# Loading the last two rows of an output projection apart on five load queues, and widening its matmuls to 512 columns

## The chip, the cores and the metric

One NeuronCore of one Trainium2 chip. The metric is device time in microseconds (us); every time quoted is a median over executions of one kernel, with their number where it matters. All differences here are below 3%, most below 1%, so each comparison uses runs of the kernel before taken on the same chip (the record names no chip for the first pair). The diffs of the experiments are shortened, and those of e6 and e7 are written against the changed kernel for reading.

## The reference, cut to what matters

Two decode steps of attention, A and B, are independent and their rows are concatenated. Each has 32 heads of 128, one query row, and an output projection `wo` of 4096 x 512 in bf16. A reads 16384 keys, B only the last 4096.

```
o = softmax(q k^T / sqrt(128)) v          # per head, one row of 128
out = o.reshape(1, 32 * 128) @ wo         # 1x4096 @ 4096x512, for A and for B
```

## The kernel before

The kernel streams 352 MB of K, V and weights through one DMA queue row (16 hardware queues, which work in parallel) and computes behind it. The change touches only the end: loading `wo` and multiplying by it. `wo`'s 4096 rows lie 32 to a partition (J = 32). A "row a partition" below is one j: 128 rows of `wo`, one on each partition, and one matmul of contraction depth 128 with a one-column weight.

```python
def _load_wo(nc, cx, st, j0, n):
    ...
    src = st.wo.rearrange("(p j) f -> p j f", j=J)
    cx.o(nc.sync.dma_start(out=st.wo_t[:, j0 : j0 + n, :], in_=src[:, j0 : j0 + n, :]))

def _fin_rows(nc, cx, sts):
    ...                                   # orow: 64 partitions, one head each; A on 0-31, B on 32-63
    for st in sts:                        # spread each head's 128 values over 4 partitions: oc_ps
        ...

def _out(nc, cx, st, j0, n):
    if j0 == 0:
        st.oc = cx.singles.tile([P, J], BF16, ...)
        cx.o(nc.vector.tensor_copy(st.oc[:, :], st.oc_ps[:, 0:J]))
    if cx.out_ps is None:
        cx.out_ps = cx.red_pool.tile([P, 2, 512], F32, tag="red", name="out_ps")
    w = st.DN // st.cols
    out = [cx.out_ps[r : r + 1, b, 0:w] for r, b in st.out_at]
    for j in range(j0, j0 + n):
        for x in range(st.cols):          # A: 1 x 512 columns; B: 2 x 256
            cx.o(nc.tensor.matmul(
                out[x], lhsT=st.oc[:, j : j + 1], rhs=st.wo_t[:, j, x * w : (x + 1) * w],
                start=(j == 0), stop=(j == J - 1),
            ))
    if j0 + n == J:
        row = ...
        cx.o(nc.vector.tensor_copy(row[0:1, 0:w], out[0]))
        if st.cols == 2:
            cx.o(nc.scalar.copy(row[0:1, w:], out[1]))
        cx.o(nc.sync.dma_start(out=cx.out[...], in_=row[0:1, :]))

# in problem():  row and bank of PSUM for the halves of the output row
st.out_at = ((0, 0),) if name == "A" else ((64, 0), (96, 1))
# pieces, in load order:  A 16, 16;  B 16, 8, 4, 2, 2
for p in pieces:
    _out(nc, cx, *p)                      # all of A, then all of B, in load order
```

The softmax here doesn't subtract the row's maximum and nothing guards it: scores larger than these inputs give would overflow.

## Time and profile before

| | before |
|---|---|
| time, median of 4 | 823.43 us (822.85 to 824.11) |
| profiled span | 821.2 us |
| DMA | 352 MB, 429 GB/s over the span |
| TensorE busy | 37% |
| last piece of B's `wo` landed | 818.16 us |
| last matmul done | 818.59 us |

From the page of the kernel before: the span, TensorE's busy share, and the row of the DMA engines' mean busy share in 40 equal slices of the span (9 is 90% or more), and the instruction fetches (packets, MB, share).

```profile
span 821.2 us, 4767 instructions
...
PE 301.1 (37%) x2148; PEld 117.3 (14%) x2148; DVE 600.7 (73%) x146; ACT 35.1 (4%) x133; POOL 1.3 (0%) x9
...
DMA  9999999999999999999999999999999999999997
...
q8 instruction: 16, 0.26, 0.1%
```

The DMA row is 9 in all slices but the last: the load stream bounds the kernel, and the change is aimed at its tail. The end of the chain of waits of the kernel before (start us, us, what) shows that tail.

```profile
789.00 29.16 DMA wo_t<-in_B_wo_dram
...
818.21 0.43 PE out_ps L307 x4
818.63 0.41 DVE rowB L316
```

The last piece of `wo` lands, four matmuls and a cast follow, then the output DMA of 1 KB. TensorE's part of the same stretch, from the timeline of the kernel before (start us, us, engine, line, operation, out<-in, shape, count, what ended the idle time before it):

```profile
803.73 8.75 PE L307 MATMUL out_ps<-wo_t,ocA 128*1 128x512 bf16 x32 [0.25 <-DVE ocA L300]
...
813.35 1.91 PE L307 MATMUL out_ps<-wo_t,ocB 128*1 128x256 bf16 x32 [0.87 <-DVE ocB L300]
...
815.69 1.04 PE L307 MATMUL out_ps<-wo_t,ocB 128*1 128x256 bf16 x16 [0.43 <-DMA wo_t<-in_B_wo_dram]
...
818.21 0.38 PE L307 MATMUL out_ps<-wo_t,ocB 128*1 128x256 bf16 x4 [0.29 <-DMA wo_t<-in_B_wo_dram]
818.62 0.42 DVE L316 CAST rowB<-out_ps 1x256 bf16<-1x256 f32 x1 [5.32 <-PE out_ps L307]
818.65 0.37 ACT L318 CAST rowB<-out_ps 1x256 bf16<-1x256 f32 x1 [15.50 <-PE out_ps L307]
```

B's 32 half-row matmuls of the first piece took 1.91 us, so a row of 512 columns costs about 0.12 us; A's 32 whole-row matmuls took 8.75 us, over a stretch in which the clock was at half for 3.4 us. And TensorE waits for a DMA before each later piece of B: it has room.

What the change aims at is visible only in the trace's record of DMA landings. A load's 16 queues each report when their share has landed. Sorted, for B's last piece in the kernel before (us):

```
814.96 815.09 815.11 815.21 815.31 815.47 815.65 815.92 | 817.77 817.88 817.92 817.98 817.99 818.10 818.10 818.16
```

Eight queues are done 1.85 us before the first of the other eight. The late half makes the kernel wait.

### The profile page before, as it was taken

The page shows a single profiled execution, that of the slowest core. Times are in us where ns is not written, and L with a number is a line of the kernel's source. Part 1 is how long each engine was busy: PE and PEld are TensorE (multiplying, and loading weights), DVE is VectorE, ACT ScalarE, POOL GpSimd, SP SyncE. Part 2 cuts the span into 40 slices and gives each one's busy share as a digit, 9 for nine tenths or more (in the row PEclk, how much of TensorE's full clock was granted, in tenths as well). Part 3 has the DMA queues.
Part 4 walks back from the last instruction along what each step waited for, and adds up shares of the span by engine and source line. Part 5 has one row for each costly group of instructions (what it writes and reads, how often), then busy time and mean ns, then how long its engine had stood idle before and what let it go on. Part 6 is the DMA issues. An engine that isn't in the chain of part 4 may idle for free.

```text
span 821.2 us, 4767 instructions
## 1 busy us (share of the span) xinstructions
PE 301.1 (37%) x2148; PEld 117.3 (14%) x2148; DVE 600.7 (73%) x146; ACT 35.1 (4%) x133; POOL 1.3 (0%) x9
## 2 busy tenths in 40 slices
PE   3433705143223415060606151423414250606076
PEld 1111202011011102020202020101101020202033
DVE  2099895997496867799196949599659677689921
ACT  0100000000010000000001000000001000000010
POOL 0000000000000000000000000000000000000000
PEclk9855668586767677675858585857666676768599
DMA  9999999999999999999999999999999999999997
GB/s 383 434 457 412 456 412 454 412 454 418 427 442 444 425 441 429 441 416 447 421 445 437 431 435 434 432 423 443 441 418 451 425 445 421 448 413 455 413 424 317
DMA packets 8235, 352.62 MB, mean 429 GB/s; under 512 B 916, under 2 KB 920, under 8 KB 1304
## 3 DMA queue, kind: packets, MB, share of 16 engines
q1 hardware_dynamic: 8212, 352.33, 99.3%
q8 instruction: 16, 0.26, 0.1%
q14 instruction: 3, 0.02, 0.0%
q10 hardware_dynamic: 4, 0.00, 0.0%
HBM read 352.32 MB, written 0.00 MB: 429 GB/s over the span
## 4 chain that ended last, share of the span: by engine, by line
DMA 61%; issue 15%; DVE 13%; PE 11%; ACT 0%; SPq 0%; DVEq 0%
DMA kt<-in_A_k_cache_dram 42%; DMA vt<-in_A_v_cache_dram 12%; PE red L190 7%; DVE kt L178 6%; DVE kt L169 4%; PE acc L231 4%; DMA vt<-in_B_v_cache_dram 4%; DMA wo_t<-in_B_wo_dram 4%; DVE sc L206 2%; ACT p_sb L212 0%; SPq L115 0%; PE out_ps L307 0%; DVE rowB L316 0%; DVEq L169 0%
## 5 line engine op out<-in xcount | busy, mean ns | idle before, releaser
L169 DVE TENSOR_TENSOR kt<-kt,qallA 128x32768 bf16<-128x32768 bf16 (+2 forms) x20 | 276.2, 13810 | 162.5 <-DMA kt<-in_A_k_cache_dram 162.5
L231 PE MATMUL acc<-vt,p_sb 128*8 128x512 bf16 (+1 forms) x1280 | 113.0, 530 | 444.4 <-ACT p_sb L212 344.4
L178 DVE TENSOR_TENSOR kt<-kt 128x16384 bf16<-128x16384 bf16 (+2 forms) x24 | 174.3, 7261 | 0.2
L190 PE MATMUL red<-kt,ident 128*128 128x512 bf16 x640 | 151.2, 396 | 54.6 <-DVE kt L178 54.6
L231 PEld LDWEIGHTS <-p_sb 128*8 128x8 bf16 (+1 forms) x1280 | 37.6, 112 | 515.7 <-ACT p_sb L212 419.8
L190 PEld LDWEIGHTS <-ident 128*128 128x128 bf16 x640 | 63.0, 101 | 142.2 <-issue 47.1
L169 DVE TENSOR_TENSOR kt<-kt,qallB 128x16384 bf16<-128x16384 bf16 x8 | 69.5, 8686 | 2.9 <-DMA kt<-in_B_k_cache_dram 2.9
L206 DVE TENSOR_REDUCE sc<-red 128x256 f32<-128x2048 f32 x20 | 45.7, 2284 | 5.6 <-PE red L190 5.6
L212 ACT ACTIVATE p_sb<-sc,offA 128x256 bf16<-128x256 f32 x32 | 16.0, 500 | 574.7 <-DVE sc L206 574.7
L245 DVE TENSOR_TENSOR acc<-acc,maskA 128x512 f32<-128x512 f32 x16 | 11.1, 694 | 21.4 <-PE acc L231 21.4
L212 ACT ACTIVATE p_sb<-sc,offB 128x128 bf16<-128x128 f32 x32 | 12.4, 388 | 161.2 <-DVE sc L206 161.2
L130 PE MATMUL q_ps<-wq_t,scr 128*128 128x512 bf16 x64 | 15.7, 407 | 6.9 <-DMA wq_t<-in_A_wq_dram 4.9
L251 DVE TENSOR_REDUCE s<-acc 128x128 f32<-128x512 f32 x24 | 16.6, 691 | 0.8
L307 PE MATMUL out_ps<-wo_t,ocA 128*1 128x512 bf16 x32 | 8.8, 443 | 0.3 <-DVE ocA L300 0.3
L245 DVE TENSOR_TENSOR acc<-acc,maskB 128x512 f32<-128x512 f32 x8 | 5.5, 692 | 4.5 <-PE acc L231 4.5
L130 PEld LDWEIGHTS <-scr 128*128 128x128 bf16 x64 | 6.5, 103 | 15.6 <-issue 8.0
L316 DVE CAST rowA<-out_ps 1x512 bf16<-1x512 f32 x1 | 0.7, 678 | 8.8 <-PE out_ps L307 8.8
L259 PE MATMUL f_ps<-s,selA 128*32 128x128 f32 x32 | 6.5, 285 | 0.0
L212 ACT ACTIVATION_READ_ACCUMULATOR p_sb<-sc,offA 128x1 f32 x32 | 6.0, 187 | 0.0
L212 ACT ACTIVATION_READ_ACCUMULATOR p_sb<-sc,offB 128x1 f32 x32 | 6.0, 186 | 0.0
L307 PE MATMUL out_ps<-wo_t,ocB 128*1 128x256 bf16 x64 | 4.3, 272 | 1.8 <-DMA wo_t<-in_B_wo_dram 0.9
L102 DVE CAST scr<-xT 128x128 bf16<-128x128 f32 (+1 forms) x6 | 2.1, 459 | 3.6 <-PE xT L94 3.5
(43 smaller groups left out, 26.4 us busy)
## 6 DMA issues: line engine op xcount, KB each, us to landing
kt<-in_B_k_cache_dram SPq DMA_DIRECT2D x8, 4096.0 KB, 32.4
vt<-in_B_v_cache_dram SPq DMA_DIRECT2D x8, 4096.0 KB, 23.8
wq_t<-in_A_wq_dram SPq DMA_DIRECT2D x1, 4096.0 KB, 12.2
wq_t<-in_B_wq_dram SPq DMA_DIRECT2D x1, 4096.0 KB
wo_t<-in_A_wo_dram SPq DMA_DIRECT2D x2, 2048.0 KB, 22.6
wo_t<-in_B_wo_dram SPq DMA_DIRECT2D x1, 2048.0 KB, 27.0
wo_t<-in_B_wo_dram SPq DMA_DIRECT2D x1, 1024.0 KB, 29.0
wo_t<-in_B_wo_dram SPq DMA_DIRECT2D x1, 512.0 KB
```

What stands on the lines that cost most here:

```text
L102: cx.o(nc.vector.tensor_copy(st.xb[:, :, g, :].rearrange("p c (i r) -> p r c i", r=R)[:, g, :, :], xT[:, :].rearrange("p (c o) -> p c o", ...
L130: cx.o(nc.tensor.matmul(q_ps[:, j, :], lhsT=st.xb[:, c, g, :], rhs=w[:, g, j * (512 // DH) : (j + 1) * (512 // DH), :], start=(g == 0 and ...
L169: cx.o(nc.vector.tensor_tensor(out=k, in0=k, in1=q.rearrange("p (o d) -> p o d", o=1).broadcast_to([P, b - a, DH]), op=ALU.mult,))
L178: cx.o(nc.vector.tensor_tensor(out=k[:, :, 0 : DH // 2], in0=k[:, :, 0 : DH // 2], in1=k[:, :, DH // 2 : DH], op=ALU.add,))
L190: cx.o(nc.tensor.matmul(load.red[:, k : k + n, :], lhsT=cx.ident[:, :], rhs=load.kt[:, k : k + n, b * W : (b + 1) * W], start=(b == 0), st ...
L206: cx.o(nc.vector.tensor_reduce(out=sc[:, :], in_=load.red[:, :, :], axis=AX.X, op=ALU.add))
L212: cx.o(nc.scalar.activation(out=u.p[:, :, g, :], in_=sc[:, u.k0 : u.k0 + n].rearrange("p (t e) -> p t e", e=4), func=ACT.Exp, scale=SCALE, ...
L231: cx.o(nc.tensor.matmul(u.acc[r : r + 4 * R, :], lhsT=u.p[:, t, :, :], rhs=u.load.vt[:, k : k + 4, :], start=(t < 4), stop=(t >= T - 4),))
L245: cx.o(nc.vector.tensor_tensor(out=acc, in0=acc, in1=st.mask[:, :].rearrange("p (x o) -> p x o", o=1).broadcast_to([P, 4, DH]), op=ALU.mult,))
L251: cx.o(nc.vector.tensor_reduce(out=u.s[:, :], in_=acc.rearrange("p x d -> p d x"), axis=AX.X, op=ALU.add,))
L259: cx.o(nc.tensor.matmul(cx.f_ps[st.f_at : st.f_at + 32, 0:DH], lhsT=st.sel[:, at : at + 32], rhs=u.s[:, :], start=(u.i == 0), stop=(u.i == ...
L307: cx.o(nc.tensor.matmul(out[x], lhsT=st.oc[:, j : j + 1], rhs=st.wo_t[:, j, x * w : (x + 1) * w], start=(j == 0), stop=(j == J - 1),))
```

## The change

The intent: take 256 KB, B's last two rows a partition, off the even spread over 16 queues and give them to queues that are early. They are loaded by eight DMAs whose outermost dimension is 5 or 3, on partitions 32 to 51, so that each head's piece lies on one partition, and multiplied there by that head's values (20 or 12 partitions deep). The part of the heads that doesn't sit on the right partitions in `orow` is moved by one small matmul. B's row becomes 512 columns a matmul, in one bank of PSUM (the memory that TensorE writes its results to), cast in two halves.

```diff
+APART = 2
+def _load_apart(nc, cx, st, part):
+    h0, k = ((0, 5), (20, 3))[part]
+    ...                                  # wo_x: [P, 2, 4, APART, 512], in a free K buffer
+    src = st.wo.rearrange("(h r j) f -> h r j f", h=H, j=J)
+    for a in range(4):
+        h = slice(h0 + a, h0 + a + 4 * k - 3, 4)
+        to = slice(st.f_at + a, st.f_at + a + 4 * k - 3, 4)
+        cx.o(nc.sync.dma_start(out=cx.wo_x[to, part], in_=src[h, :, J - APART : J, :]))
 ...                                      # _fin_rows: one matmul and one cast make oc_x from orow
-    for j in range(j0, j0 + n):
-        for x in range(st.cols):
-            ...                          # two halves, rows 64 and 96, banks 0 and 1
+    out = cx.out_ps[row : row + 1, bank, :]
+    todo = [(st.oc[:, j : j + 1], st.wo_t[:, j, :]) for j in range(j0, j0 + n)]
+    if st.apart and j0 + n == st.apart_at:              # after B's first 16 rows
+        for part, (oc, k) in enumerate(((st.oc_x[0], 20), (st.oc_x[1], 12))):
+            h = slice(st.f_at, st.f_at + k)
+            todo += [(oc[h, r, j : j + 1], cx.wo_x[h, part, r, j, :])
+                     for r in range(DH // J) for j in range(st.apart)]
+    for i, (o, wo) in enumerate(todo):
+        cx.o(nc.tensor.matmul(out, lhsT=o, rhs=wo, start=..., stop=...))
 ...
+        cx.o(nc.vector.tensor_copy(row[0:1, 0:w], out[:, 0:w]))
+        cx.o(nc.scalar.copy(row[0:1, w:], out[:, w:]))
-        st.out_at = ((0, 0),) if name == "A" else ((64, 0), (96, 1))
+        st.out_at = (0, 0) if name == "A" else (64, 1)
-    for x in (J // 2, J // 4, J // 8, J // 16, J // 16):
+    for x in (J // 2, 9, 4, 1):          # and a part of wo_x after each of A's two pieces
```

More of the change, by code (lines that the diff above doesn't have):

```diff
@@ L146, in _load_wo @@
     cx.o(nc.sync.dma_start(out=st.wo_t[:, j0 : j0 + n, :], in_=src[:, j0 : j0 + n, :]))
+def _load_apart(nc, cx, st, part):
+    J = st.wo.shape[0] // P
+    H = st.wo.shape[0] // DH
+    n = DH // J
+    h0, k = ((0, 5), (20, 3))[part]
+    if part == 0:
+        cx.wo_x = cx.kt_pool.tile([P, 2, n, APART, st.DN], BF16, tag="kt", name="wo_x")
+    src = st.wo.rearrange("(h r j) f -> h r j f", h=H, j=J)
[3 more added lines that the diff above has]
+        cx.o(nc.sync.dma_start(out=cx.wo_x[to, part], in_=src[h, :, J - APART : J, :]))
 def _load_kv(nc, cx, load, which, tag):
@@ L282, in _fin_rows @@
         J = st.wo.shape[0] // P
+        if st.apart:
+            ends = orow[:, :].rearrange("p (r j) -> p r j", j=J)[:, :, J - st.apart : J]
+            h = st.f_at + 20
+            cx.out_ps = cx.red_pool.tile([P, 3, 512], F32, tag="red", name="out_ps")
+            moved = cx.out_ps[0 : P - 20, 2, 0 : DH // J * st.apart].rearrange("p (r j) -> p r j", j=st.apart)
+            cx.o(nc.tensor.matmul(
+                moved, lhsT=cx.ident[st.f_at : st.f_at + H, 20:P], rhs=ends[st.f_at : st.f_at + H],
+                start=True, stop=True, skip_group_check=True,
+            ))
+            oc = cx.small.tile([P, DH // J, st.apart], BF16, tag="oc_x", name="oc_x")
+            cx.o(nc.vector.tensor_copy(oc[0 : P - 20], moved))
+            st.oc_x = (ends, oc)
         n = DH // J
@@ L300, in _out @@
         cx.o(nc.vector.tensor_copy(st.oc[:, :], st.oc_ps[:, 0:J]))
-    if cx.out_ps is None:
-        cx.out_ps = cx.red_pool.tile([P, 2, 512], F32, tag="red", name="out_ps")
-    w = st.DN // st.cols
-    out = [cx.out_ps[r : r + 1, b, 0:w] for r, b in st.out_at]
-    for j in range(j0, j0 + n):
-        for x in range(st.cols):
-            cx.o(nc.tensor.matmul(
-                out[x],
-                lhsT=st.oc[:, j : j + 1],
-                rhs=st.wo_t[:, j, x * w : (x + 1) * w],
-                start=(j == 0),
-                stop=(j == J - 1),
-            ))
-    if j0 + n == J:
+    w = st.DN // 2
+    row, bank = st.out_at
+    out = cx.out_ps[row : row + 1, bank, :]
[3 more added lines that the diff above has]
+            h = slice(st.f_at, st.f_at + k)
+            todo += [
+                (oc[h, r, j : j + 1], cx.wo_x[h, part, r, j, :])
+                for r in range(DH // J) for j in range(st.apart)
+            ]
+    last = j0 + n == J - st.apart
+    for i, (o, wo) in enumerate(todo):
+        cx.o(nc.tensor.matmul(
+            out, lhsT=o, rhs=wo, start=(j0 == 0 and i == 0), stop=(last and i == len(todo) - 1),
+        ))
+    if last:
         row = cx.accs_pool.tile([1, st.DN], BF16, tag="accs", name=f"row{st.name}")
-        cx.o(nc.vector.tensor_copy(row[0:1, 0:w], out[0]))
-        if st.cols == 2:
-            cx.o(nc.scalar.copy(row[0:1, w:], out[1]))
+        cx.o(nc.vector.tensor_copy(row[0:1, 0:w], out[:, 0:w]))
+        cx.o(nc.scalar.copy(row[0:1, w:], out[:, w:]))
         cx.o(nc.sync.dma_start(out=cx.out[0, 0:1, st.at : st.at + st.DN], in_=row[0:1, :]))
@@ L373, in problem @@
         st.v_view = v_cache[0, :, sk0 : sk0 + W, :]
-        st.out_at = ((0, 0),) if name == "A" else ((64, 0), (96, 1))
-        st.cols = len(st.out_at)
+        st.out_at = (0, 0) if name == "A" else (64, 1)
+        st.apart, st.apart_at = (0, 0) if name == "A" else (APART, 16)
         st.f_at = 0 if name == "A" else 32
@@ L407 @@
         ld.add(None if i else "vt", lambda p=p: _load_wo(nc, cx, *p))
+        if i < 2:
+            ld.add(None if i else "kt", lambda i=i: _load_apart(nc, cx, stB, i))
     ld.pump()
```

## The prediction

> **What bounds the kernel now.** The load stream: the DMA row is 9 in all 40 slices but the last, 352 MB at 429 GB/s over 821.2 us; TensorE is busy 37%. The chain of waits ends with "DMA wo_t<-in_B_wo_dram" until 818.16, then four matmuls (0.43), a cast (0.41), the output DMA. So only the tail can move. In the trace's DMA landings the 16 queues of one load do not finish together: for each of the last loads eight of them land 1.8 us or more after the other eight (B's last piece: 814.96-815.92 against 817.77-818.10). The 16 instruction fetches of 16 KB (about 0.95 us each, one queue at a time) look like the cause: each leaves one more queue behind. The tiny output DMA of row A lands at 815.26, before the late eight, so the queue it used is among the early ones.
>
> **The change's DMA half.** 256 KB (B's last two rows a partition) leave the even spread, 16 KB a queue, and go in eight DMAs whose outer dimension is 5 or 3. "DMA: Bandwidth & Descriptors", "Why a DMA increments its semaphore by 16", says such a DMA uses as many queues as divide that dimension, the lowest-numbered: so queues 0-4 get 32 KB and 0-2 another 32 KB (no run shows it yet). The late eight carry 16 KB less. B's last two pieces, 16 KB a queue each, landed 0.61 us apart, so B's wo should be complete about 0.6 us earlier, near 817.5. The loaded queues gain at most 48 KB, 1.8 us, about the gap. The SP queue must issue 13 loads instead of 7 (0.4-0.6 us each, some waiting for the load eight before them); I estimate all in time.
>
> **The change's TensorE half.** Before, B's row was two 256-column matmuls on output rows 64 and 96; in the timeline both start within 4 ns and the pairs follow at 0.109 us. "TensorE: Matmul & The Clock Gate", Part 3, says matmuls in distinct column groups run concurrently; the trace agrees. After, one 512-column matmul in one column group: A's row shows that form at 0.216 us a matmul (full clock), 0.427 at half. So a row of B costs 0.216 instead of 0.109. And the 256 KB, two full rows before, become 16 matmuls of 20 or 12 partitions, which still stream 512 columns each. B's matmuls: 32 x 0.109 = 3.5 us before, 46 x 0.216 = 9.9 us after.
>
> B can't start earlier: its first 16 rows land at 813.22, and A's matmuls hold TensorE until 812.5. Estimate: 813.3 + 16 x 0.216 = 816.7; the 16 apart to 820.2; 9 + 4 rows to 823.0; last one done near 823.4; 0.1-0.3 for switching between full and 32-partition matmuls. Before it was done at 818.59. So TensorE, not the load, ends last: +4.9 us. The 0.6 us from the loads is hidden. One extra matmul and cast before A's rows (0.2 us) and the halved cast of row A change nothing there.
>
> **Predicted**: 823.3 + 4.9 = 828.2 us, 8 in 10 between 827.0 and 829.6. Faster by over 2%: 0.01; within 2%: 0.98; slower by over 2%: 0.01.
>
> **What shows it.** wo landings end near 817.5; TensorE runs without a gap from about 813.3 to 823.4; B's matmuls at 0.216 us; the chain's tail names TensorE's out_ps line, some 6 us, instead of the B wo DMA.
>
> **What would make it wrong.** 20-row matmuls overlapping or costing less than 0.216 us (then near 824-825). Clock granted at half late in B's matmuls (up to +2). Loads starved because issues wait on earlier loads, or the chosen queues being the late ones (wo later, but TensorE still hides some 5 us).

## The result, and the profile after

The changed kernel took 828.88 us (median of 4, 828.39 to 830.22) against 823.43: ratio 1.0068, 95% interval 1.0051 to 1.0086. (Ratios are the mean time of one kernel's runs over that of the other's of the same rounds, so not quite the ratio of the medians.) The execution profiled was the 830.22 one. From its page, the same rows:

```profile
span 828.5 us, 4744 instructions
...
DMA  9999999999999999999999999999999999999994
...
q8 instruction: 16, 0.26, 0.1%
```

The end of its chain of waits:

```profile
805.19 8.18 DMA wo_t<-in_B_wo_dram
...
813.41 11.97 PE out_ps L342 x46
...
825.46 0.43 DVE rowB L347
...
825.91 0.37 ACT rowB L348
```

The chain no longer ends on a load. From the moment that B's first piece has landed, 46 matmuls follow one another for 12 us, then two casts one after the other. TensorE in the timeline:

```profile
813.41 3.61 PE L342 MATMUL out_ps<-wo_t,ocB 128*1 128x512 bf16 x16 [1.25 <-DMA wo_t<-in_B_wo_dram]
816.95 1.88 PE L342 MATMUL out_ps<-wo_x,orow 20*1 20x512 bf16 x8
818.68 1.89 PE L342 MATMUL out_ps<-wo_x,oc_x 12*1 12x512 bf16 x8
820.50 4.87 PE L342 MATMUL out_ps<-wo_t,ocB 128*1 128x512 bf16 x14
```

Start to start is 0.2157 us within the first three groups, and 0.31 and 0.30 us at the two turns between full and short matmuls. In the last group 9 matmuls are 0.29 to 0.43 us apart, because the granted clock fell to half at 820.99 for 3.41 us. The columns of the stretches are: us from:to, length, busy time and number of instructions of each engine, granted clock (TensorE's, 1.00 is full and 0.50 half), DMA share, GB/s.

```profile
817.00:820.00 3.00, 3.00 (x16) 1.08 (x16) 0.00 (x0) 0.00 (x0) 0.00 (x0) 1.00 0.02 6
820.00:825.00 5.00, 5.00 (x17) 1.50 (x15) 0.00 (x0) 0.00 (x0) 0.00 (x0) 0.66 0.00 0
```

The load part did what it was made for. The landings of B's last piece after:

```
816.58 816.66 816.66 816.67 816.70 817.01 817.04 817.21 817.23 817.28 817.31 817.37 817.38 817.46 817.47 817.71
```

All 16 queues are done within 1.1 us of each other, where it had been 3.2 us, and the last is 0.45 us earlier than before. But TensorE finishes 7.65 us after that.

The sum, for the profiled executions (span 821.2 to 828.5, so +7.3): the last matmul is done at 825.36 instead of 818.59, +6.77, of which the half clock is 1.69 (the last 14 matmuls start over 4.49 us, where 13 steps of 0.2157 would be 2.80). From the end of the last matmul to the end of the casts it is 0.92 instead of 0.45, +0.47. Without the half clock it is 5.08 + 0.47 = 5.55 us, which is what the three faster executions show (828.39, 828.69 and 829.06, 5.0 to 5.6 over the median before).

### The profile page after: what moved, and what is told of

Read it like the earlier page. It is cut to its first block, busy times and chain, and to the rows that moved or that the text cites. A ratio compares the mean times of both kernels' runs of the same rounds, so it can differ in the third digit from the quotient of the medians.

```text
span 828.5 us, 4744 instructions
## 1 busy us (share of the span) xinstructions
PE 304.1 (37%) x2131; PEld 117.5 (14%) x2131; DVE 600.5 (72%) x147; ACT 35.5 (4%) x134; POOL 1.3 (0%) x9
## 4 chain that ended last, share of the span: by engine, by line
DMA 60%; issue 15%; PE 12%; DVE 11%; ACT 1%; SPq 0%; DVEq 0%
DMA kt<-in_A_k_cache_dram 41%; DMA vt<-in_A_v_cache_dram 15%; PE red L206 6%; PE acc L247 5%; DVE kt L194 5%; DVE kt L185 4%; DMA wo_t<-in_A_wo_dram 2%; DVE sc L222 2%; PE out_ps L342 1%; DMA wo_t<-in_B_wo_dram 1%; ACT p_sb L228 1%; SPq L162 0%; SPq L116 0%; DVE rowB L347 0%; ACT rowB L348 0%
## 5 line engine op out<-in xcount | busy, mean ns | idle before, releaser
L247 PE MATMUL acc<-vt,p_sb 128*8 128x512 bf16 (+1 forms) x1280 | 110.7, 521 | 445.0 <-ACT p_sb L228 344.8
L206 PE MATMUL red<-kt,ident 128*128 128x512 bf16 x640 | 149.1, 392 | 57.8 <-DVE kt L194 57.8
L342 PE MATMUL out_ps<-wo_t,ocB 128*1 128x512 bf16 x30 | 8.5, 447 | 1.2 <-DMA wo_t<-in_B_wo_dram 1.2
```

The source lines that it names most:

```text
L206: cx.o(nc.tensor.matmul(load.red[:, k : k + n, :], lhsT=cx.ident[:, :], rhs=load.kt[:, k : k + n, b * W : (b + 1) * W], start=(b == 0), st ...
L247: cx.o(nc.tensor.matmul(u.acc[r : r + 4 * R, :], lhsT=u.p[:, t, :, :], rhs=u.load.vt[:, k : k + 4, :], start=(t < 4), stop=(t >= T - 4),))
L342: cx.o(nc.tensor.matmul(out, lhsT=o, rhs=wo, start=(j0 == 0 and i == 0), stop=(last and i == len(todo) - 1),))
```

## The experiments

Theory T: the loss is TensorE's column streaming. A whole row in one column group (output row 64 lies in one, row 96 in another) costs 0.216 us where two half rows side by side cost 0.109, and the 16 short matmuls cost as much as full ones. Rival R: the loss is in the loads (14 issues instead of 7, short pieces, uneven queues; the trace shows six loads to `wo_t` and eight to `wo_x`). Two questions came with it: why the clock fell to half (C: short-partition matmuls don't keep it up; W: chance of the windows), and why one half of the queues is late (F: instruction fetches).

### r1_after: the changed kernel again

No edit.

> The changed kernel again, unedited, beside the next three. All theories: about 5.4 us over the kernel before. In the profile taken of it first, the granted clock fell to half from 820.99 for 3.4 us, which stretched 8 of B's last matmuls from 0.216 to 0.427 us (about 1.7 us), and that execution took 830.22 us against 828.39 to 829.06 for the three others. If that throttling is a matter of where the clock's windows fall, other executions lack it and the median stays near 828.8; the profile here may or may not show it.

Measured: five executions at 828.77, 830.09, 832.22, 832.22 and 832.35, beside 823.38 before; ratio 1.0092. The profile is of the 830.09 one and repeats the first to a few hundredths: half clock at 820.99 for 3.41 us, 0.66 in the same stretch. So the expectation that the median stays at 828.8 missed. The changed kernel has three levels, near 828.6, 830.1 and 832.2, and which it takes varies from job to job. The steps of 1.6 and 2.1 us are of the size that half clock in the last matmuls gives, but both profiles are of the 830 level; neither the 828.6 nor the 832 level was profiled.

### e1_pairs: only the column change undone

```diff
-        st.out_at = (0, 0) if name == "A" else (64, 1)
+        st.out_at = ((0, 0),) if name == "A" else ((64, 1), (96, 0))
     for i, (o, wo) in enumerate(todo):
-        matmul(out, lhsT=o, rhs=wo)
+        for x in range(len(out)):
+            matmul(out[x], lhsT=o, rhs=wo[:, x * wide : (x + 1) * wide])
```

> The change with its loads kept, but B's row again as two 256-column matmuls on output rows 64 and 96 (also for the rows loaded apart). Theory T (TensorE's column streaming is the loss): pairs at 0.109 us, so 46 rows cost 5.0 us instead of 9.9; B's matmuls end near 818.9, the two casts run side by side again, and the time is within 0.7 us of the kernel before (823.4 plus 0.3). Rival R (the loss is in the loads: 13 issues instead of 7, short transfers, queues unevenly loaded): stays near 828.9.

Measured: 823.92 (823.19 to 824.27), ratio to before 1.0003 (0.999 to 1.0015). The end of its chain:

```profile
805.15 8.39 PE out_ps L343 x32
...
813.56 0.41 DVE rowA L349
813.97 0.11 DVE ocB L328
...
814.13 0.27 PE out_ps L343
...
814.42 5.41 PE out_ps L343 x91
```

With all loads of the change kept, the whole loss is gone: R falls, T stands. All 46 rows take 5.7 us from 814.13 instead of 12. TensorE still ends last, because in this execution A's row met the half clock and B's small cast waits behind A's: that is where the earlier landing of the last load (817.85 here) goes.

### e2_512_alone: only the column change

The loads as in the kernel before, five pieces and nothing apart; B's row as 512 columns in one bank.

```diff
-        st.apart, st.apart_at = (0, 0) if name == "A" else (APART, 16)
+        st.apart, st.apart_at = 0, 0
-    for x in (J // 2, 9, 4, 1):
+    for x in (J // 2, J // 4, J // 8, J // 16, J // 16):     # and no load apart
```

> The kernel before in its loads (five pieces of B's wo, nothing apart), with only B's row as 512 columns a matmul and one output bank. Theory T: 32 matmuls at 0.216 us from 813.3 end near 820.5 instead of 818.6, and the two casts of the row run one after the other (0.4 us), so 2.2 to 2.5 us over the kernel before, about 825.7. Rival R: as the kernel before, 823.4.

Measured: 825.38 (825.20 to 825.59), ratio 1.0022 (1.001 to 1.0035). The end of the chain:

```profile
785.80 27.57 DMA wo_t<-in_B_wo_dram
...
813.41 7.08 PE out_ps L344 x32
...
820.57 0.43 DVE rowB L349
...
821.02 0.36 ACT rowB L350
```

With the loads as they were, the wide row alone costs 2.0 us by the medians, and 2.3 by the spans of the profiled executions (823.5 and 821.2): 32 matmuls in 7.08 us end 1.9 us later than before, and the two casts stand one after the other here too, 0.4 us more. In e1, with the halves in two banks, they start 0.02 us apart (819.88 and 819.90), as they do in the kernel before. The rows apart account for 3.2 of the change's remaining 3.5 us: 16 matmuls (3.45 us) where two rows had been, which is two matmuls (0.43) in this form, plus the two turns between full and short matmuls (0.31 and 0.30 us between starts instead of 0.216).

### e3_apart_first: the rows apart before B's first rows

```diff
-            todo += [ ...rows apart... ]
+            first += [ ...rows apart... ]
+    todo = first + todo
```

> The change with one move: the 16 matmuls of the rows loaded apart come before B's first 16 rows, in the 1.4 us in which TensorE waited for those rows (812.0 to 813.4). Theory T: since TensorE ends last, every microsecond of waiting filled comes back: 1.0 to 1.4 us less than the changed kernel, about 827.6. Rival R: no change, 828.9.

Measured: 827.96 (827.05 to 828.88), ratio 1.0051. The profiled one (828.88) gave the gain back before the rows apart: A's row met the half clock from 804.89 to 808.30 and ended at 813.91 instead of 812.16, so there was no waiting left to fill. In its chain TensorE works without a break for 18.6 us:

```profile
805.44 18.59 PE out_ps L344 x78
```

The two fastest executions, 827.05 and 827.22, lie 0.4 to 0.6 us below the 827.6 expected, the median as much above it. It agrees with T, but alone it would not decide, as its range touches the changed kernel's. One thing in this trace matters for the clock. The same 16 short matmuls in a row, here from 813.84 to 817.38, did not bring it down: it stayed full from 808.30 to 828.78. Two stretches after the short ones:

```profile
817.00:820.00 3.00, 3.00 (x16) 1.04 (x14) 0.00 (x0) 0.00 (x0) 0.00 (x0) 1.00 0.12 43
820.00:825.00 5.00, 4.01 (x19) 1.40 (x17) 0.42 (x1) 0.36 (x1) 0.00 (x0) 1.00 0.00 0
```

### e4_apart_thrice and e5_full_thrice: what short-partition matmuls do to the clock

Their outputs are wrong, which doesn't matter for the times. e4 does the 16 short matmuls three times; e5 does 48 matmuls of the same width over all 128 partitions in their place.

```diff
 e4: -  for r in range(DH // J) for j in range(st.apart)
     +  for x in range(3) for r in range(DH // J) for j in range(st.apart)
 e5, besides: -  (oc[h, r, j : j + 1], cx.wo_x[h, part, r, j, :])
              +  (st.oc[:, 2 * r + j : 2 * r + j + 1], st.wo_t[:, 2 * r + j, :])
```

> Wrong result on purpose: the 16 matmuls of 20 or 12 partitions are each done three times. Theory C (the clock's monitor counts such short-partition matmuls as little activity): in the 10.4 us that they take, the granted clock falls to half while TensorE is never idle, and some matmuls take 0.427 us; time 6.9 us (32 x 0.216) over the changed kernel plus some microseconds, 837 to 841. Rival W (only a matter of where windows fall, or of idle time earlier): full clock through that stretch, 835.8.

> Wrong result on purpose: as the run before it, but the 48 matmuls read all 128 partitions of B's first rows, so the same count and the same columns. Theory C: the clock stays at full speed until the end, 6.9 us over the changed kernel, about 835.7, and less than the run before it by the time lost at half clock. Rival W: the same as the run before it.

Measured: e4 844.05 (4 executions, 842.57 to 844.32), above the 837 to 841 expected, because the clock stayed down longer; e5 835.40 (835.19 to 835.45), as expected. TensorE in the timeline of e4, where it is never idle:

```profile
817.20 7.21 PE L342 MATMUL out_ps<-wo_x,orow 20*1 20x512 bf16 x24
824.20 10.44 PE L342 MATMUL out_ps<-wo_x,oc_x 12*1 12x512 bf16 x24
834.57 4.64 PE L342 MATMUL out_ps<-wo_t,ocB 128*1 128x512 bf16 x14
```

The stretches of e4 that tell it, then those of e5 (granted clock is the third number from the end):

```profile
817.00:820.00 3.00, 3.00 (x15) 1.03 (x14) 0.00 (x0) 0.00 (x0) 0.00 (x0) 1.00 0.03 11
820.00:834.00 14.00, 14.00 (x35) 4.05 (x34) 0.00 (x0) 0.00 (x0) 0.00 (x0) 0.52 0.00 1
```

```profile
817.00:820.00 3.00, 3.00 (x15) 1.18 (x14) 0.00 (x0) 0.00 (x0) 0.00 (x0) 1.00 0.03 12
820.00:828.00 8.00, 8.00 (x39) 3.11 (x37) 0.00 (x0) 0.00 (x0) 0.00 (x0) 1.00 0.01 2
```

The clock of e4 falls to half at 820.50, 3.3 us after the short matmuls begin, and comes back at 837.56, 3.0 us after the full ones resume. That of e5 stays full until its last matmul. The 8.65 us between them are what half clock costs: 14.07 us of short matmuls from 820.50 to 834.57 and 2.99 after them, half of each, 8.5 us. C stands and W falls for 48 such matmuls in a row. For the 16 of the changed kernel (3.54 us) the record is mixed: the clock fell in both of its profiles and not in e3's, so where they fall in the clock's windows may count as well. The Trainium skill, "TensorE: Matmul & The Clock Gate", Part 1, describes the gate as following TensorE's activity in windows of about 3.4 us; the trace agrees, the pieces at half clock are multiples of 3.41 us. It does not say that a matmul of 20 or 12 partitions leaves the gate closing.

### e11_full_once: the same in the changed kernel's own size

The 16 short matmuls (of 20 or 12 partitions) replaced by 16 full ones, once (e5's second edit alone; wrong result).

> Wrong result on purpose: the changed kernel, its 16 matmuls of 20 or 12 partitions replaced by 16 over all 128 partitions of B's first rows; count, columns and loads as in the changed kernel. Its nine executions so far spread from 828.39 to 832.35. Theory C (short-partition matmuls let the clock fall): all executions here lie within 0.6 us of each other, near 828.3, and the clock stays full to the end of B's row. Rival: the same spread up to 830 and 832 remains.

Measured: 828.53, 828.83, 828.84, 829.00 and one 830.32, ratio 1.007. The profiled one has full clock from 799.1 to 826.4. None of the five is at 832, where three of the changed kernel's nine were, but five are few. Four of them lie within 0.5 us and one does not, so the expectation held only in part: a step of 1.5 us has another cause too. That execution has no profile, and the cause stays open. Half clock in A's row, as in the kernel before and in e3, would hardly do: in e11's profile TensorE waits 0.74 us within A's row and 1.90 us before B's first rows, together more than the 1.7 us that half clock costs. It also puts a number on columns and casts without the half clock: in the profiled execution (828.84, full clock through A's and B's rows) the loss is 5.6 us, of which some tenths belong to B's first piece, which landed at 813.86 instead of 813.37.

### e8_more_fetches: why half of the queues is late

The kernel before, with 54 tiny matmuls whose result is not used after the work on each of 20 loads: 2160 more TensorE instructions, in its idle time.

```diff
+        for _ in range(54):
+            matmul(stA.oc_ps[0:32, 64:72], lhsT=cx.ident[:, 0:32], rhs=cx.ident[:, 0:8])
```

> The kernel before with 54 tiny matmuls (8 columns, result unused) after each of the 20 loads' folds, 2160 instructions more, in TensorE's idle time. Theory F (the late eight queues are late because TensorE's instruction fetches of 16 KB go through them, 16 of them, two a queue): the profile shows about 24 fetches, the late eight land about 1.2 us later still against the early eight, and the time is about 1.2 us over the kernel before, 824.6. Rival (the halves differ for another reason, such as the memory they read): the gap between the halves stays at 1.8 us and the time within 0.4 us.

Measured: 825.72 (825.53 to 826.10), ratio 1.0034 (1.002 to 1.0047), in a job where before took 822.96. That is 2.8 us over it, more than twice the 1.2 expected. Its page's line of instruction fetches, and the end of its chain:

```profile
q8 instruction: 25, 0.41, 0.2%
```

```profile
790.27 30.49 DMA wo_t<-in_B_wo_dram
...
820.80 0.43 PE out_ps L307 x4
821.22 0.41 DVE rowB L316
```

25 fetches instead of 16. The gap between the halves of B's last piece (eight landings by 816.07, the next at 819.25) is 3.2 us instead of 1.85, 1.3 more where 1.2 was expected. The very last landing, at 820.76, is another 1.05 us behind the one before it, after the 25th fetch at 814.0; 24 had been expected. F stands: in this run, e9 and e10 a fetch of 16 KB sets one queue back by 1.0 to 1.4 us, and here the early eight (last landing 816.07, before 815.92) carry none. The Trainium skill, "Runtime: NRT & Kernel Launch", "Instruction fetch mechanics", gives blocks of 16 KiB, 256 instructions, and calls the cost of crossing one mostly hidden. The trace agrees with the block (2160 more instructions, 9 more fetches of 16 KB); in a kernel that waits for its loads the cost is not hidden, 2.8 us here.

### e6_eight_queues and e7_eight_queues_4: a variant of my own, and what it got wrong

Both: four DMAs of 8 heads (outermost dimension 8) in place of the eight of 5 or 3, so no moved part; A's and B's rows as pairs of 256 columns; the rows apart before B's first. e6 takes 2 rows a partition apart, e7 takes 4.

```diff
-    h0, k = ((0, 5), (20, 3))[part]
+    k = 8                       # heads a, a+4, ... a+28 on partitions 32+a, 36+a, ... 60+a
-APART = 2
+APART = 4                       # e7; pieces of B then 16, 8, 3, 1
```

> The idea of the change with the TensorE cost taken away: B's last 2 rows a partition in four DMAs of 8 heads (so queues 0 to 7, 32 KB each), one partition a head, 8 small matmul pairs instead of 16 single ones, done before B's first rows; A's and B's rows both as two 256-column matmuls side by side. Theory T: TensorE no longer ends last, the late queues carry 16 KB less, so 0.4 to 0.6 us under the kernel before, 822.9. Rival R: slower than before.

> The same with B's last 4 rows a partition apart (64 KB on each of queues 0 to 7, 32 KB less on the late eight). Theory T: 0.9 to 1.2 us under the kernel before, about 822.3, with both halves of the queues finishing within some 0.5 us. Rival R: slower than before. If the gain is less than in the run before it, the early queues have become the late ones.

Measured: e6 824.21 (823.54 to 825.90), ratio 1.0011 (0.9997 to 1.0025); e7 823.85 (7 executions, 823.72 to 828.38), ratio 1.0007. No gain, against both expectations. The profile of e7 is of its slowest execution, 828.38, 3.2 us above the next. The landings of its first DMA apart point to why:

```
801.23 801.26 801.31 801.85 801.94 802.17 | 804.16 804.18
```

Of the eight queues used, two land 2 us after the six others: they are not the early half. The first DMA apart of e6 shows the same (six by 802.37, two at 804.38 and 804.41). In the changed kernel the five landings of its first DMA are 800.67, 800.70, 801.15, 801.15 and 801.60, all early. So I had put more on two queues that were already late, and B's last piece landed at 819.45 in e6 and 819.52 in e7 instead of 818.16. The number of landings, 5, 3 and 8, agrees with the Trainium skill, "DMA: Bandwidth & Descriptors" ("Why a DMA increments its semaphore by 16 and not by 1"); that they are the lowest-numbered queues no run here shows. That landing alone rules out a gain in these two executions, but their chains end on TensorE. That of e6:

```profile
795.84 14.42 DMA wo_t<-in_A_wo_dram
...
810.30 2.51 PE out_ps L331 x32
...
815.15 5.02 PE out_ps L331 x58
```

The two late queues delayed A's second piece too (810.25 in e6, 808.37 in the kernel before), TensorE waited 2.99 us for it, and the clock was at half from 811.49 to 818.32; in e7 it was at half from 809.82 to 823.48. How much each of these costs is not separated, and the faster executions of e7 have no profile.

### e9_apart_between and e10_all_pairs_warm: can the loads' gain be kept?

e9: the change's loads; B's row and the rows apart in pairs; the rows apart between A's two halves; B's small cast moved ahead. e10: A in pairs too, and 12 unused full matmuls before B's rows to keep the clock up.

```diff
     _row(nc, cx, st, rows, last)            # pairs on rows 64 and 96, banks 1 and 2
+    if st.name == "A" and j0 == 0:
+        _apart(nc, cx, cx.stB)
 e10: A's row on rows 0 and 32; before B's first rows
+        for x in range(12):
+            matmul(cx.out_ps[0:1, 3, :], lhsT=st.oc[:, 0:1], rhs=cx.wo_t[:, 0, x, :])
```

> The change's loads, B's row and the rows apart as pairs of 256 columns, the pairs of the rows apart moved between A's two halves (A's row stays at 512 columns), B's small cast moved ahead of A's matmuls. The loads of the change landed at 817.7 against 818.1 before, and e1 lost it because TensorE reached B's first rows 0.7 us late and still had the rows apart behind them. Expected: B's first rows start at 813.4 to 815, TensorE catches up with the last load, and the time is 0 to 0.4 us under the kernel before; if TensorE still ends last, up to 0.3 us over it.

> As the run before it, with A's row too in pairs of 256 columns, and 12 matmuls over all 128 partitions whose result is not used put before B's rows, so that TensorE is not idle while B's rows arrive (in e6 and e7, where TensorE was idle there, the clock fell to half). Expected: full clock from about 808 on, B's rows done 0.2 us after the last load near 817.7, time 0.3 to 0.5 us under the kernel before. If an instruction fetch falls into the last microseconds on a queue that is late, that gain is gone.

Measured, before at 823.14: e9 822.67 (822.47, 822.63, 822.67, 823.68, 824.24), ratio 0.9997 (0.9983 to 1.0011); e10 823.67 (823.60 to 824.39), ratio 1.0009. Neither is shown to beat the kernel before. The end of e9's chain, in the 824.24 execution, the slowest of its five:

```profile
806.02 12.89 DMA wo_t<-in_B_wo_dram
...
818.95 0.75 PE out_ps L332 x10
```

TensorE is no longer the end: the load is, at 818.91. The landings of the last piece are fifteen by 817.62 and one at 819.06. A 17th instruction fetch at 816.92, which the kernel before doesn't have (it stops at 16), had set one queue back by 1.4 us. The pairs add 58 instructions to TensorE's stream against the kernel before, and that is enough to reach the next block. In e10 the 17th fetch fell at 813.6 and one queue landed at 818.69 against 817.70 for the fifteen others. So the gain that the loads give, 0.45 us in one profile, is smaller than the 1.0 to 1.4 us that one fetch costs its queue, and the instructions that keep TensorE off the end bring that fetch. Three of e9's five executions, 822.47 to 822.67, were below all nine of the kernel before in that job (822.90 to 823.24); they have no profile, and whether that gain is real stays open.

## Why the prediction was right, and where it was off

**The bound moves from the loads to TensorE**: right. The chain ends on 46 matmuls from 813.41 instead of a load, and e1 takes the loss away by the column form alone.

**B's start at 813.3, 0.216 us a matmul, the short ones no cheaper**: right. 813.41; 0.2157 for 128, 20 and 12 partitions alike; 3.61 us for the first 16, 3.5 for the 16 short ones. The rows of 9, 4 and 1 began at 820.50 (predicted 820.2 and 0.1 to 0.3 for switching). Without the half clock the last is done at 823.67 (predicted 823.4 and 0.1 to 0.3).

**The pairs run side by side before**: right, as the Trainium skill has it ("TensorE: Matmul & The Clock Gate", Part 3). In the kernel before the two halves start within 4 ns and pairs follow at 0.109 us; undone in e2, that costs 2.0 us together with the casts.

**The loads gain 0.6 us, hidden**: right in kind, and 0.45 us in size (818.16 to 817.71). That is one pair of profiles: in the six with the change's loads and no late fetch before the last landing (the change, r1, e3, e4, e5, e11) the last landing lies between 817.57 and 818.24, in the two with the old loads (before, e2) at 818.16 and 818.28, so the gain is 0 to 0.6 us. The 14 issues (the prediction counted 13) were in time: B's first piece was issued only at 805.19, because issues waited for loads before them, and still landed at 813.37, 0.15 us later than before.

**The term that was mis-sized**: the end after the last matmul, taken as unchanged. The prediction spoke of A's halved cast and did not see that B's two casts now read one PSUM bank on one partition and run one after the other: 0.92 us instead of 0.45. The Trainium skill, "PSUM — Partial Sum Buffer", "PSUM bank collisions raise a hardware error", had it: two engines must not access one bank of the same partitions at once, reads included, so something has to order them. The trace agrees, ScalarE's cast is released by VectorE's (start to start 0.45 us, against 0.02 to 0.03 with two banks); I had not looked it up. That is most of the difference between +4.9 predicted and the +5.45 of the medians.

**The half clock "late in B's matmuls (up to +2)"**: named as what could make the prediction wrong, and it does occur, in both profiles of the changed kernel, 1.69 us. The prediction had no reason for it; e4 and e5 gave one that holds for a longer run of short matmuls. Of the nine executions of the changed kernel five, one in the first job and four in the second, lie above the range of 827.0 to 829.6. The range held for the median of the first job, and not for that of the second: which level the first job drew was luck. What puts an execution at 832 was not profiled and stays open; e11's five executions without it are too few to decide.

## What to carry to other kernels

When a load-bound kernel's tail is rearranged, count the other engines in that tail anew: TensorE had 37% busy over the span and was still the end once its columns stopped running side by side. A matmul here cost its columns whatever its depth (0.2157 us at 128, 20 and 12 partitions), so splitting a row of weights over fewer partitions multiplied TensorE's time, and a long run of such matmuls dropped the clock as well. Look at the landings of each queue before giving queues different amounts, and at the number of instruction fetches before adding instructions.

## What the Trainium skill lacked or had wrong

- "TensorE: Matmul & The Clock Gate", Part 1, ties the clock to TensorE's activity but not to how many partitions a matmul uses. Matmuls of 20 and 12 partitions, back to back, let the clock fall to half after 3.3 us and held it there for 14 us; matmuls of the same width over 128 partitions in the same place did not (844.05 against 835.40 us). That was 48 in a row; 16 in a row did so in two profiles of three.
- "Runtime: NRT & Kernel Launch", "Instruction fetch mechanics", calls the cost of a block crossing mostly hidden. It says nothing of the loads that share a queue with the fetch. In this load-bound kernel a 16 KB fetch set one load queue back by 1.0 to 1.4 us, and nine more of them cost 2.8 us.
- No page says which load queues carry the instruction fetches. Here it is eight of 16: by their landings, none of the five that a DMA with outermost dimension 5 uses, and two of the eight that one of dimension 8 uses. The eight are late by 1.85 us at the end of the kernel.
